# A retention layer feeding a squared-ReLU FFN on one core: the first four chunks and the first two weight pieces in another order

## The chip, the cores and the metric

The kernel runs on one core of one Trainium2 chip. The metric is the device time of one execution in microseconds (us), from the median of several runs. Everything below about engines comes from one profiled execution of that core: TensorE (PE, with its weight loads shown apart as PEld), VectorE (DVE), ScalarE (ACT), GpSimd (POOL), and SyncE (SP), which here only issues DMAs.

## What is computed

For 8 batches of 8 heads, 576 positions and head size 64, the reference computes retention without a softmax, and sends the result through a two-layer network:

```python
scores = (1/sqrt(64)) * q @ k.T                      # per batch and head
D[s, t] = gamma[h] ** (s - t) if s >= t else 0       # gamma[h] = 1 - 2 ** (-5 - h)
ret = (scores * D) @ v                               # (8, 8, 576, 64)
x = ret.transpose(0, 2, 1, 3).reshape(4608, 512)
h = maximum(x @ w_in, 0)                             # w_in (512, 2048)
out = (h * h) @ w_out                                # w_out (2048, 512)
```

q, k and v are float32. The two weights arrive as float64, so each must be turned into float32 on the chip before it is of use.

## The kernel before, in words

**Chunks.** The 4608 rows of x are made in 36 chunks of 128 rows (`C`). For each chunk q, k and v are loaded; q and v are multiplied by powers of gamma (`scale_q`, `scale_v`); q and k are turned around on PE by products with the identity (`turn_in`, L434) and copied out of PSUM by ACT or DVE (`turn_out`, L448, the copies on L454). `scores_full` (L503) makes the 128x128 scores of the eight heads with PE (L509) and multiplies them by the causal mask on DVE, one instruction for each half of the heads (L513); `carry_full` (L520) adds what earlier chunks left in a state (L529); `retain_full` (L532) multiplies the masked scores by v (L535) and k by v for the next state (L538), after which ACT copies the state (L501) and the chunk's x (L550). That is the form of chunks 0 to 3, the only ones that the change names. They are written out by hand at the end of the kernel, L853 to L914; the later ones run in the loop at L915. Each engine executes its own instructions in the order in which this Python text issues them, and so does the SP queue its DMAs. Nothing is reordered by a planner.

**Weight pieces.** w_in is cut into 16 pieces of 512x128. A piece comes in as 512 KB of raw float64 (`fetch_w`, L205; `fetch_raw(n)` fetches the next n, at most eight ahead), and is made float32 by six steps (`round_parts`, L219): *one* (L227), *two* (L231), *three* (L238), *four* (L241) and *five* (L244) on DVE, and *beside* (L235) on ACT, which needs *one* and is needed by *four*. `convert(n)` issues the next n of these steps, wherever the previous call stopped, in the order one, two, beside, three, four, five.

**The FFN of block 0.** Four chunks make a block of 512 rows. For block 0 the first layer is computed plainly: `first_in(j, halves, at)` (L667) multiplies piece j by the chosen rows of x (L677, four contraction steps, each of which shows as two PE instructions), ACT applies the ReLU (L683), and the square is queued: on ACT (L685) when both halves of the rows are taken, on DVE (L687) when only one is; `some(2)` in the next `first_in` issues it. Piece 0 is taken in four quarters of 128 rows, each as soon as a chunk's x is there; `N_HALF` says how many pieces are taken other than whole. What is left of block 0 waits in the list `steps`, and `step()` runs the next one. All other blocks go through seven products in place of eight (L717), and the second layer does likewise (L1061).

**Queues and buffers around the change.** In L152 to L158 a chunk's q and k come in two DMAs each (even heads, odd heads; 128 KB each), its v in one. Nearly all DMAs are issued from SP; `issue` (L149) sends k and v of chunk 0 through ACT's queue. PSUM holds a pool of three banks (tag f) that scores, first-layer products and warming products share in rotation, two banks for the turned q and k of the early chunks, one tile for x (`x_ps`, with one buffer, so that the next chunk's `carry_full` waits until L550 has read it) and one for the state. `warm(n)` issues products of no use into an f bank.

The order before, from L854 on, cut to its core:

```python
scale_q(1, nc.vector, halves); load(3); fetch_raw(3); warm(1)
scores_full(0); turn(1, (0, 0)); carry_full(0); retain_full(0); convert(3)
scores_full(1); scale_q(2, nc.gpsimd); carry_full(1); retain_full(1); convert(3)
turn(2, (0, 0)); load(4); ...; first_in(0, (0,), (0, C))
scores_full(2); scale_q(3, nc.gpsimd); carry_full(2); turn(3); retain_full(2)
```

Piece 0 was fetched earlier, at L345, between chunk 1's k and v; `load(2)` follows it.

Of the kernel before, what the change touches and what calls it, by code (L numbers as in the profile page):

```python
# [15 lines left out]
C = 128  # L16
CH = C // 2
TOK = 512
HT = TOK // 2
# [22 lines left out]
def kernel(  # L42
# [33 lines left out]
    nc = tc.nc  # L76
# [3 lines left out]
    HP = H // 2  # L80
# [59 lines left out]
    def load(i, names="qkv"):  # L140
        if i == 0:
            nc.sync.dma_start(dv, decays)
        got = loaded.setdefault(i, [None] * 3)
        for name, pool, src in (("q", ld3, q), ("k", ld5, k), ("v", ld4, v)):
            if name not in names:
                continue
            t = got["qkv".index(name)] = pool.tile([128, H, D], F32, tag=name, name=f"{name}_ld")

            issue = nc.scalar if i == 0 and name != "q" else nc.sync  # L149
            b, c0 = divmod(i * C, S)  # L150
            runs = [(b, c0, slice(0, C))] if c0 + C <= S else [(b, c0, slice(0, CH)), (b + 1, 0, slice(CH, C))]
            for e in range(1 if name == "v" else 2):  # L152
                for b, c0, to in runs:
                    at = src[b, :, c0:c0 + to.stop - to.start, :].rearrange("h s d -> s h d")
                    if name == "v":
                        issue.dma_start(t[to], at)
                    else:
                        issue.dma_start(t[to, e * HP:(e + 1) * HP, :], at[:, e::2, :])  # L158
# [5 lines left out]
    pieces = [(0, m, e) for m in range(N_M) for e in range(2)]  # L164
    pieces += [(1, mq + mh * N_MQ, e) for mq in range(N_MQ) for mh in range(2) for e in range(2)]
    N_W1 = N_DF
    N_HALF = 1
    stage = [W[5].rearrange("p (o s f) -> p o s f", o=4, s=NP),
             W[6][:, 0:3 * NP * 128].rearrange("p (o s f) -> p o s f", o=3, s=NP)]
    N_RAW = 8  # L170
# [11 lines left out]
    def rows(half, n=64):  # L182
        return slice(64 * half, 64 * half + n)
# [21 lines left out]
    def fetch_w(j):  # L205
        if j < len(pieces) and wide:
            to = raw_of(j).bitcast(I64)
            if pieces[j][0] == 0:
                nc.sync.dma_start(to.rearrange("p (c f) -> p c f", c=N_DM), piece_src(j))
                return  # L210
            to = to.rearrange("p (o s b c) -> o s p b c", o=2, s=2, b=4)
            for o in range(2):
                for s in range(2):
                    nc.sync.dma_start(to[o, s], piece_src(j)[o, s])
# [94 lines left out]
    def fetch_raw(count):  # L309

        for _ in range(count):
            if n_raw[0] < min(N_W1, n_made[0] + N_RAW):
                fetch_w(n_raw[0])
                n_raw[0] += 1
# [18 lines left out]
    def convert(count):  # L333
        for _ in range(count):
            f = next(w_in_steps, None)
            f and f()
# [44 lines left out]
    HEADS = [(hp, e, hp // (HP // 2)) for hp in range(HP) for e in range(2)]  # L381
# [10 lines left out]
    def scale_q(i, engine, parts=(slice(0, H),)):  # L392
        at = N_PAT + i % N_PAT
        for heads in parts:
            t = loaded[i][0][:, heads, :]
            engine.tensor_tensor(t, t, dv[:, heads, at:at + 1].to_broadcast(list(t.shape)), op=ALU.mult)  # L396
# [8 lines left out]
    def new_qk(i):  # L405
        t = work3.tile([128, 2, HP, C], F32, tag="qk", name="qk")
        st[i]["qT"], st[i]["kT"] = t[:, 0, :, :], t[:, 1, :, :]
        return t
# [22 lines left out]
            nc.scalar.copy(*moves.pop(0)[2:])  # L431
            count -= 1

    def turn_in(i, js=(1, 0)):  # L434

        if "p" not in st[i]:
            if i < N_EARLY:
                p = [ps_e.tile([128, 512], F32, tag=f"e{h}", name="t_ps") for h in range(2)]
            else:
                p = [ps_f.tile([128, 512], F32, tag="f", name="t_ps") for h in range(2)]  # L440
            st[i]["p"] = [x.rearrange("p (j d t) -> p j d t", j=2, d=HP) for x in p]
        for j in js:
            for hp in range(HP):
                for h in range(2):
                    nc.tensor.transpose(st[i]["p"][h][:, j, hp, :], loaded[i][j][rows(h), 2 * hp:2 * hp + 2, :],  # L445
                                        ident[rows(h), rows(h)])

    def turn_out(i, engines=(0, 1)):  # L448

        p = st[i].pop("p")  # L450
        to = new_qk(i)
        copies = (nc.scalar.copy, nc.vector.tensor_copy)
        for h in range(2):
            copies[engines[h]](to[:, :, :, CH * h:CH * h + CH], p[h])  # L454

    def turn(i, engines=(0, 1)):
        turn_in(i)
        turn_out(i, engines)
# [61 lines left out]
    def carry_full(i):  # L520

        xp[0] = ps_x.tile([128, 2, 256], F32, tag="x", name="x_ps", padded_shape=[128, 2, 512])
        clean.clear()
        if i == 0:
            u_ps[0] = ps_u.tile([128, HP, D], F32, tag="u", name="u_ps")
            return
        u = u_sb[2 * i % 3]
        for hp, e, b in HEADS[0:2] + HEADS[4:6] + HEADS[2:4] + HEADS[6:8]:
            nc.tensor.matmul(x_full(hp, e, b), lhsT=u[rows(e), hp, :], rhs=st[i]["qT"][rows(e), hp, :],  # L529
                             start=clears(b, e), stop=False, skip_group_check=True)  # L530

    def retain_full(i):  # L532

        for hp, e, b in (HEADS[j] for j in (0, 4, 2, 6, 1, 5, 3, 7)):
            nc.tensor.matmul(x_full(hp, e, b), lhsT=st[i]["vs"][:, head(hp, e), :], rhs=st[i]["ret"][:, e, hp, :],  # L535
                             start=clears(b, e), stop=False, skip_group_check=True)
        for hp, e, b in HEADS:
            nc.tensor.matmul(u_ps[0][rows(e), hp, :], lhsT=loaded[i][1][:, 2 * hp + e, :], rhs=st[i]["vs"][:, head(hp, e), :],  # L538
                             start=(i == 0 and hp == 0), stop=(hp == HP - 1), skip_group_check=True)
        x_out(i, lambda: grown(i, 1))  # L540
# [126 lines left out]
    def first_in(j, halves=(0, 1), at=(0, HT)):  # L667

        assert n_made[0] > j
        wi, m, e = pieces[j]  # L670
        mp, mm = divmod(m, 2)
        p = ps_f.tile([128, 2, HT], F32, tag="f", name="h_ps")
        w = w_in[mp][:, mm, 2 * e:2 * e + 2, :, :].rearrange("p s c f -> p (s c) f")
        lo, hi = halves[0], halves[-1] + 1
        p = p[:, lo:hi, at[0]:at[1]]
        for c in range(N_DM):
            nc.tensor.matmul(p, lhsT=w[:, c, :], rhs=xT[0][:, c, :].rearrange("p (h t) -> p h t", h=2)[:, lo:hi, at[0]:at[1]],  # L677
                             start=(c == 0), stop=(c == N_DM - 1))

        t = g_room[mp % 2][:, 2:5:2, mm, :] if e else g_room[mp % 2][:, 0:4:3, mm, :]  # L680
        t = t[:, lo:hi, at[0]:at[1]]
        some(2)
        nc.scalar.activation(t, p, AF.Relu)  # L683
        if hi - lo == 2:
            queue.append(lambda: nc.scalar.activation(t, t, AF.Square))  # L685
        else:
            queue.append(lambda: nc.vector.tensor_tensor(t, t, t, op=ALU.mult))  # L687
        if mm and e and hi == 2 and at[1] == HT:
            queue.append(lambda: [nc.sync.dma_start(
                g_dram[0, a:b, :, 2 * mp:2 * mp + 2, :].rearrange("s p m t -> p s (m t)"),  # L690
                g_room[mp % 2][:, a:b, :, :].rearrange("p s m t -> p s (m t)")) for a, b in QUARTERS])
        if j >= N_W1 - 4:

            sums_w.setdefault(0, sum_w_in(0)).pop(0)()
            if n_next[0] > 1:
                if 1 not in sums_x:
                    sums_x[1] = sum_x(1)
                sums_x[1].pop(0)()
# [89 lines left out]

    def block_steps(n):
        if n == 0:  # L790
            seconds = [(0, first_in, j, (1,), (C, HT)) for j in range(N_HALF)]
            return seconds + [(0, first_in, j) for j in range(N_HALF, N_W1)]
        return [(n, ffn_in, n, mp, j) for mp in range(N_MP) for j in range(NP)]

# [58 lines left out]
    halves = (slice(0, HP), slice(HP, H))  # L853
# [3 lines left out]
    scale_v(0)  # L857
    turn_in(0, (0,))
    turn_out(0)
    scale_q(1, nc.vector, halves)  # L860
    load(3)
    fetch_raw(3)
    warm(1)
    scores_full(0)
    turn(1, (0, 0))
    carry_full(0)
    retain_full(0)
    convert(3)
    scores_full(1)
    scale_q(2, nc.gpsimd)  # L870
    carry_full(1)
    retain_full(1)
    convert(3)
    turn(2, (0, 0))
    load(4)
    load(5, "qk")
# [3 lines left out]
    first_in(0, (0,), (0, C))  # L880
    scores_full(2)
    scale_q(3, nc.gpsimd)
    carry_full(2)
    turn(3)
    retain_full(2)
    load(6)
    fetch_raw(1)
    convert(3)
    scores_full(3)
    scale_q(4, nc.gpsimd)  # L890
    carry_full(3)
    first_in(0, (0,), (C, HT))
    early.close()
    ps_t[0] = first.enter_context(tc.tile_pool(name="ps_t", bufs=1, space=PS))
    convert(3)
    retain_full(3)
    first_in(0, (1,), (0, C))
    convert(6)
    scale_v(4)
    step()  # L900
    step()
# [239 lines left out]
    for k in range(N_K + 1):  # L1141
        j = k % NP
# [81 lines left out]
```

## Time and profile before

| what | value |
|---|---|
| median of three runs | 931.96 us (931.69 to 932.58) |
| the profiled execution's own time | 931.9 us |
| its span, first to last instruction | 930.2 us |
| PE busy | 922.4 us, 99% of the span |
| DVE busy | 755.4 us, 81% |
| ACT busy | 346.2 us, 37% |
| POOL busy | 82.9 us, 9% |
| granted PE clock | 0.999 of full |
| PE busy from 5.68 to 17.00 us | 9.75 of 11.32 us |
| PE busy from 17.00 to 31.40 us | 14.40 of 14.40 us |

The busy share of PE counts an instruction from its start to its modelled end; products overlap, so start-to-start distances say more than sums of durations. In the timeline a line gives the start, the time covered, the engine, the source line, the operation, what it writes and reads, shape, count, and in brackets the idle time of the engine ahead of it with what ended it. In the table of DMA issues the last column is the time from issue to landing.

### The profile page before, as it was taken

The numbers are of one execution on the slowest core, as the hardware profiler recorded it, in microseconds if no ns is written. First come the engines' busy times: TensorE is split into PE (matmuls) and PEld (weight loads), VectorE is DVE, ScalarE is ACT, GpSimd is POOL, SyncE is SP. The second block draws the span as 40 slices with busy tenths as digits, with TensorE's granted clock in tenths as the row PEclk, the third lists the DMA queues.
The fourth block names the chain that finished last, engine by engine and source line by source line (L and its number), as shares of the span: only waits on it lengthen the run. The fifth ranks groups of instructions, "written<-read, shape, count | busy, mean of one in ns | idle before, by whom it ended". The sixth has DMA issues, their size and how long they took to land.

```text
span 930.2 us, 21072 instructions
## 1 busy us (share of the span) xinstructions
PE 922.4 (99%) x8548; PEld 830.2 (89%) x8548; DVE 755.4 (81%) x1215; ACT 346.2 (37%) x788; POOL 82.9 (9%) x82
## 2 busy tenths in 40 slices
PE   8999999999999999999999999999999999999997
PEld 7654888888888888888888899999999999999997
DVE  5888788888898888979876587888888888877877
ACT  3457767667676676676711110000000000000000
POOL 3222111011111111211000000000000000000000
PEclk9999999999999999999999999999999999999999
DMA  9998657578666775784379996566666575465523
GB/s 226 220 270 218 166 153 202 161 214 267 167 180 184 259 216 146 223 271 137 114 258 355 383 318 193 145 176 191 168 180 183 156 206 155 114 178 142 151 79 68
DMA packets 297376, 181.29 MB, mean 195 GB/s; under 512 B 194368, under 2 KB 270272, under 8 KB 296384
## 3 DMA queue, kind: packets, MB, share of 16 engines
q1 hardware_dynamic: 292208, 178.84, 66.5%
q10 hardware_dynamic: 5072, 1.12, 0.6%
q8 instruction: 67, 1.10, 0.5%
q14 instruction: 29, 0.24, 0.1%
HBM read 109.39 MB, written 70.52 MB: 193 GB/s over the span
## 4 chain that ended last, share of the span: by engine, by line
PE 98%; DVE 1%; DMA 1%; SPq 0%; issue 0%; ACT 0%; DVEq 0%
PE h_b L717 18%; PE o_b L1061 18%; PE h_a L717 12%; PE h_c L717 12%; PE o_c L1061 12%; PE o_a L1061 12%; PE h_ps L677 6%; PE x_ps L574 3%; PE sc_ps L480 2%; PE x_ps L609 1%; PE u_ps L568 1%; DMA q_ld<-in_q_dram 1%; PE sc_ps L509 0%; PE t_ps L445 0%; PE x_ps L535 0%; DVE room L513 0%
## 5 line engine op out<-in xcount | busy, mean ns | idle before, releaser
L717 PE MATMUL h_b<-room,w 128*128 128x256 f32 x768 | 181.4, 379 | 0.0
L431 ACT COPY qk<-flip 32x256 f32<-32x256 f32 x432 | 173.8, 402 | 6.7
L717 PEld LDWEIGHTS h_b<-room,w 128*128 128x128 f32 x768 | 145.9, 190 | 19.8
L717 PE MATMUL h_a<-room,w 128*128 128x256 f32 x512 | 123.9, 385 | 0.0
L717 PE MATMUL h_c<-room,w 128*128 128x256 f32 x512 | 121.0, 379 | 0.0
L717 PEld LDWEIGHTS h_c<-room,w 128*128 128x128 f32 x512 | 97.3, 190 | 13.2
L717 PEld LDWEIGHTS h_a<-room,w 128*128 128x128 f32 x512 | 95.0, 190 | 13.7
L1061 PE MATMUL o_b<-room,w 128*128 128x192 f32 x496 | 90.8, 326 | 0.0
L1074 ACT COPY r<-o_a 128x192 f32<-128x192 f32 x28 | 8.9, 319 | 209.4 <-PE o_a L1061 209.4
L1061 PEld LDWEIGHTS o_b<-room,w 128*128 128x128 f32 x496 | 82.3, 190 | 0.0
L724 DVE SCALAR_TENSOR_TENSOR room<-room 128x512 f32<-128x512 f32 x96 | 66.7, 695 | 3.3
L396 POOL TENSOR_TENSOR q_ld<-q_ld,dv 128x512 f32<-128x512 f32 x34 | 37.7, 1110 | 286.1 <-DMA q_ld<-in_q_dram 257.2
L1061 PE MATMUL o_a<-a,w 128*128 128x192 f32 x352 | 62.6, 326 | 0.0
L1061 PE MATMUL o_c<-room,w 128*128 128x192 f32 x336 | 61.5, 326 | 0.0
L1061 PE MATMUL o_b<-s,w 128*128 128x192 f32 x336 | 61.5, 326 | 0.0
L1061 PE MATMUL o_c<-s,w 128*128 128x192 f32 x336 | 61.5, 326 | 0.0
L677 PE MATMUL h_ps<-room,w 128*128 128x512 f32 (+1 forms) x152 | 57.7, 532 | 0.7 <-DVE w L244 0.6
L1061 PEld LDWEIGHTS o_a<-a,w 128*128 128x128 f32 x352 | 58.1, 190 | 0.1
L1061 PE MATMUL o_a<-room,w 128*128 128x192 f32 x320 | 56.9, 326 | 0.0
L1061 PEld LDWEIGHTS o_c<-room,w 128*128 128x128 f32 x336 | 55.8, 190 | 0.0
L1061 PEld LDWEIGHTS o_b<-s,w 128*128 128x128 f32 x336 | 55.8, 190 | 0.0
L1061 PEld LDWEIGHTS o_c<-s,w 128*128 128x128 f32 x336 | 55.8, 190 | 0.0
(116 smaller groups left out, 1409.2 us busy)
## 6 DMA issues: line engine op xcount, KB each, us to landing
g_dram<-room SPq DMA_DIRECT2D x164, 256.0 KB, 3.8
a<-g_dram SPq DMA_DIRECT2D x30, 512.0 KB, 5.3
room<-g_dram SPq DMA_DIRECT2D x28, 512.0 KB, 5.0
w_dram<-w SPq DMA_DIRECT2D x28, 448.0 KB, 4.5
w<-w_dram SPq DMA_DIRECT2D x7, 1792.0 KB, 9.8
q_ld<-in_q_dram SPq DMA_DIRECT2D x64, 128.0 KB, 4.1
w<-in_moe_w_in_dram SPq DMA_DIRECT2D x16, 512.0 KB, 6.3
w<-in_moe_w_out_dram SPq DMA_DIRECT2D x64, 128.0 KB, 3.4
```

The source lines that it names most:

```text
L396: engine.tensor_tensor(t, t, dv[:, heads, at:at + 1].to_broadcast(list(t.shape)), op=ALU.mult)
L431: nc.scalar.copy(*moves.pop(0)[2:])
L480: nc.tensor.matmul(st[i]["sc"][e][rows(h), hp, :], lhsT=st[i]["kT"][rows(e), hp, t], rhs=st[i]["qT"][rows(e), hp, t], start=True, stop=Tru ...
L568: return [lambda hp=hp, e=e, b=b: nc.tensor.matmul(u[rows(e), hp, :], lhsT=loaded[i][1][rows(h), 2 * hp + e, :], rhs=st[i]["vs"][rows(h), ...
L574: return [lambda hp=hp, e=e, b=b: nc.tensor.matmul(x_at(hp, e, b, h), lhsT=s["vs"][rows(h), head(hp, e), :], rhs=s["ret"][rows(h), e, hp, ...
L609: m = nc.tensor.matmul(x_at(hp, e, b, h), lhsT=u[rows(e), hp, :], rhs=s["qT"][rows(e), hp, CH * h:CH * h + CH], start=clears(b, e), stop=F ...
L677: nc.tensor.matmul(p, lhsT=w[:, c, :], rhs=xT[0][:, c, :].rearrange("p (h t) -> p h t", h=2)[:, lo:hi, at[0]:at[1]], start=(c == 0), stop= ...
L717: nc.tensor.matmul(p[:, mm, :], lhsT=w[:, c, :], rhs=xs[n][right][:, c, :], start=(j in OPENS and mm == 0 and c == 0), stop=(j in CLOSES a ...
L724: nc.vector.scalar_tensor_tensor(t, t, 0.0, t, op0=ALU.max, op1=ALU.mult)
L1061: nc.tensor.matmul(p, lhsT=w_out[j][:, m, WO_SLOT[right], :], rhs=s["lefts"][left][:, m, :], start=(i in OPENS and m == 0), stop=(i in CLO ...
L1074: nc.scalar.copy(r[:, 0, LEFT], p)
```

## The change

1. Chunk 0's q is issued from ACT's queue and its k and v from SP's; before, it was the other way round.
2. Chunk 1's q is scaled half on DVE and half on GpSimd; before, both halves on DVE.
3. The raw piece 1 is fetched ahead of chunk 3's q, k and v; before, behind them. Pieces 2 and 3 stay behind.
4. Chunk 1's first half of the heads is turned around right after chunk 0's scores; the second half inside `retain_full(0)`, between the four products of the even heads and the four of the odd ones. Its copies are split between ACT and DVE; before, both on ACT.
5. Of piece 0, *one*, *two*, *beside* and *three* are issued inside `retain_full(0)` too, *four* and *five* after the mask of chunk 1.
6. All six steps of piece 1 are issued after the mask of chunk 2, ahead of `carry_full(2)`. Before, they came after the mask of chunk 3 and later.
7. Piece 0's second quarter goes between `carry_full(2)` and `retain_full(2)`; chunk 3 is turned around after `retain_full(2)`; piece 1 is used in two halves of 256 rows, the first ahead of `scores_full(3)`, the second as a step at the end; piece 0's third quarter goes ahead of `retain_full(3)`.

```diff
-            issue = nc.scalar if i == 0 and name != "q" else nc.sync
+            issue = nc.scalar if i == 0 and name == "q" else nc.sync
...
-    N_HALF = 1
+    N_HALF = 2
...
-    def turn_in(i, js=(1, 0)):
+    def turn_in(i, js=(1, 0), hps=range(HP)):
...
-            for hp in range(HP):
+            for hp in hps:
...
-    def retain_full(i):
-
-        for hp, e, b in (HEADS[j] for j in (0, 4, 2, 6, 1, 5, 3, 7)):
+    def retain_full(i, inside=lambda: None):
+
+        for j in (0, 4, 2, 6, 1, 5, 3, 7):
+            hp, e, b = HEADS[j]
+            if j == 1:
+                inside()
...
-            seconds = [(0, first_in, j, (1,), (C, HT)) for j in range(N_HALF)]
+            seconds = [(0, first_in, 0, (1,), (C, HT))] + [(0, first_in, j, (1,)) for j in range(1, N_HALF)]
...
-    scale_q(1, nc.vector, halves)
+    scale_q(1, nc.vector, halves[:1])
+    scale_q(1, nc.gpsimd, halves[1:])
+    fetch_raw(1)
     load(3)
-    fetch_raw(3)
+    fetch_raw(2)
     warm(1)
     scores_full(0)
-    turn(1, (0, 0))
+    turn_in(1, (1, 0), (0, 1))
     carry_full(0)
-    retain_full(0)
-    convert(3)
+    retain_full(0, lambda: [turn_in(1, (1, 0), (2, 3)), turn_out(1), convert(4)])
     scores_full(1)
     scale_q(2, nc.gpsimd)
+    convert(2)
     carry_full(1)
     retain_full(1)
-    convert(3)
     turn(2, (0, 0))
...
     scores_full(2)
     scale_q(3, nc.gpsimd)
+    convert(6)
     carry_full(2)
+    first_in(0, (0,), (C, HT))
+    retain_full(2)
     turn(3)
-    retain_full(2)
     load(6)
     fetch_raw(1)
-    convert(3)
+    first_in(1, (0,))
     scores_full(3)
     scale_q(4, nc.gpsimd)
+    convert(3)
     carry_full(3)
-    first_in(0, (0,), (C, HT))
+    first_in(0, (1,), (0, C))
     early.close()
...
     convert(3)
     retain_full(3)
-    first_in(0, (1,), (0, C))
-    convert(6)
     scale_v(4)
     step()
     step()
```

## The prediction, made before the changed kernel was run

> **What bounds the kernel now.** I read the page's busy times first, then PE's waits, then the timelines of PE, DVE, POOL and ACT over the first 55 us, and the DMA issues there.
>
> ```profile
> PE 922.4 (99%) x8548; PEld 830.2 (89%) x8548; DVE 755.4 (81%) x1215; ACT 346.2 (37%) x788; POOL 82.9 (9%) x82
> ```
>
> PE is the bound. PE's waits over the whole span, the four that the view lists (total, times, longest):
>
> ```profile
> PE idle_ps L845 <- DVE w L342: 1.1, 1, 1.1
> PE h_ps L677 <- DVE w L244: 0.6, 1, 0.6
> PE x_ps L535 <- DVE room L513: 0.4, 2, 0.3
> PE sc_ps L509 <- DVE qk L454: 0.3, 1, 0.3
> ```
>
> All of them lie ahead of 17 us. So whatever moves the start of the first step after the changed stretch, `turn(4)`, moves the end by as much, as long as no new wait appears behind it. PE's timeline gives the marks:
>
> ```profile
> 13.74 1.16 PE L535 MATMUL x_ps<-room,v_ld 128*64 128x128 f32 x16 [0.27 <-DVE room L513]
> 14.74 0.64 PE L538 MATMUL u_ps<-v_ld,k_ld 128*64 128x64 f32 x16
> 15.30 0.46 PE L445 MATMUL t_ps<-w,k_ld 64*128 64x64 f32 x8
> 15.60 0.41 PE L445 MATMUL t_ps<-w,q_ld 64*128 64x64 f32 x8
> 16.63 1.16 PE L677 MATMUL h_ps<-room,w 128*128 128x128 f32 x8 [0.61 <-DVE w L244]
> 17.71 1.16 PE L509 MATMUL sc_ps<-qk 64*128 64x128 f32 x16
> ...
> 31.41 0.46 PE L445 MATMUL t_ps<-w,k_ld 64*128 64x64 f32 x8
> ```
>
> The start of chunk 2's turning is 15.30, the one stall worth having is the 0.61 ahead of piece 0's first quarter (16.63, waiting for *five*, L244), and `turn(4)` starts at 31.41. Start to start, from this timeline: turning 0.65, scores 1.09, carry 0.60, a quarter of a piece 1.09, products with v 0.92, state 0.57; three groups (two quarters and a whole piece) take 25.80 to 31.41, so a whole piece is 5.61 - 2.18 = 3.43 and a half about 1.72.
>
> DVE, POOL and ACT show what a conversion costs undisturbed and disturbed:
>
> ```profile
> 28.01 1.06 POOL L396 TENSOR_TENSOR q_ld<-q_ld,dv 128x512 f32<-128x512 f32 x1 [7.36 <-DVE w L238]
> ```
>
> ```profile
> 18.91 1.29 DVE L513 TENSOR_TENSOR room<-sc_ps,room 128x512 f32<-128x512 f32 x2 [2.34 <-PE sc_ps L509]
> ...
> 28.05 1.57 DVE L241 SCALAR_TENSOR_TENSOR w<-w,w 128x512 f32<-128x512 f32 x1
> ...
> 49.38 0.41 DVE L227 TENSOR_SCALAR w<-w 128x512 uint32<-128x512 uint32 x1
> ...
> 51.69 0.69 DVE L244 SCALAR_TENSOR_TENSOR w<-w,w 128x512 uint32<-128x512 uint32 x1
> ```
>
> From 49.38 to 52.38 one piece takes 3.00 us with POOL idle. At 28.05 *four* takes 1.57 in place of 0.69, because POOL began at 28.01: it ends 0.55 after POOL does. The mask at 18.91 keeps its 1.29 although POOL works from 19.59 on.
>
> [...] It also shows a *one* (L227, 56.59) at 0.93 in place of 0.42 beside POOL, so I take all five DVE steps to be exposed. [...] issue to landing is 5 to 6 us from the fourth microsecond on, so the engines have a backlog and bytes decide. [...]
>
> **Part by part.**
>
> *q first, and chunk 1 around chunk 0 (edits 1, 2, 4).* In the landing times (start of the issue plus the last column of the DMA issues), chunk 0's k lands at 3.69 and 5.31, its q at 5.05 and 6.03, and the scaling (0.42) follows the last q. With q first, the scaling runs before k is complete. Bytes up to the last needed landing fall a little, and I expect the copies at 6.6 instead of 6.91, and chunk 1's scores at 11.3 instead of 11.71. SP gets one DMA more to issue (0.53 on ACT's queue); behind a backlog of 5 us that costs nothing, without the backlog 0.5 on everything from SP. But two things take the gain back before chunk 2. First, *beside* of piece 0 now stands on ACT ahead of the state copy and the x copy. It needs *one*, which needs piece 0: issued at 5.06, landed 5.9 later at 10.93.
>
> ```profile
> w<-in_moe_w_in_dram SPq DMA_DIRECT2D x1, 512.0 KB, 5.9
> ```
>
> *One* from 11.05 to 11.47, then on ACT 0.61 for *beside*, 0.27 and 0.59: x is read by 12.98, and `carry_full(1)`, which needs that PSUM tile, starts at 13.07, where chunk 1's scores were over at 12.4. After 0.60 of carry, chunk 1's products start at 13.7 as they do now. Second, chunk 2's second half of k is issued at 10.75 and takes this long:
>
> ```profile
> k_ld<-in_k_dram SPq DMA_DIRECT2D x1, 128.0 KB, 4.5
> ```
>
> That is 15.24; PE turns chunk 2 at 15.30 now. Nothing ahead of it in the byte order changes, so **chunk 2 is turned at 15.3 again**. These edits are worth 0 here (bounds: a gain of 0.2, since the first half of k2 is there at 13.9; a loss of 0.5 if SP's issues slip).
>
> *Piece 0 sooner (edit 5).* *Three* moves ahead of chunk 1's mask; behind the mask (13.9) come *four* and *five*, 0.7 each, with `scale_q(2)` on POOL until about 14.7: done at 15.95, where PE gets there. The quarter starts at 16.03: **-0.60**. Scores of chunk 2 need ACT's copies of the turned chunk, over at 17.25 as now (16.16 + 1.09): they start at 17.3, 0.41 earlier than 17.71. Carry 18.4, second quarter 19.0, products with v 20.1, state 21.0, turning of chunk 3 21.6, **PE reaches piece 1 at 22.2**.
>
> *Piece 1 ahead of chunk 3 (edit 3).* v of chunk 2 lands at 16.32. Now chunk 3 follows (q to 17.36, k to 18.51, v 19.52), then piece 1 (21.49, that is 1.97 for 512 KB). After: piece 1 at 18.3, q 19.3, k 20.5, v 21.5. k is in time for 21.6. But `scale_q(3)` and `scale_v(3)` on POOL, now at 17.52 and 19.59, move to 19.4-20.5 and 21.6-22.6.
>
> *Piece 1's conversion (edit 6).* Its six steps stand on DVE behind chunk 2's mask, which starts 1.20 after the scores (18.91 - 17.71) and lasts 1.27: 18.5 to 19.8. From there 3.00 undisturbed would end at 22.8. Both POOL instructions now fall inside: *one* starts at 19.8 while POOL works until 20.5 (+0.55), and `scale_v(3)` slips in between *three* and *four* (+0.88, as at 28.05). Piece 1 is ready at **24.2**, and PE waits from 22.2 to 24.25: **+2.05**. Bounds: both collisions missed 0.6, one 1.2, both with a bad start 2.4. On DVE the second copy of chunk 3 and chunk 3's mask are queued behind it; PE comes to them later than DVE does.
>
> *Piece 1 by halves (edit 7).* 2 x 1.72 against 3.43: 0 (bounds 0 and +0.3). Its squares go to DVE, two of some 0.45, and leave ACT (0.64). The rest of the edit is a new order of the same PE work.
>
> **Sum.** From piece 1 on: half 1.72, scores 1.09, carry 0.60, quarter 1.09, v 0.92, state 0.57, quarter 1.09, half 1.72 = 8.80. 24.25 + 8.80 = 33.05 for `turn(4)`, against 31.41: **+1.64**. Behind that, piece 2 is ready near 32.4 to 33.0 (mask of chunk 3 over at 28.4, 3.0 of conversion, one square, one or two collisions); PE wants it at 33.7. Later pieces have 1.0 to 4 us of slack and DVE has gaps (0.41, 0.88) to catch up. The profiled execution's own time is 931.9 (930.2 of span and 1.7 around it; the median is 931.96), so 931.9 + 1.64 = 933.5; I say **933.6**, in favour of small waits left out. That is slower, but by a hair under 0.2% (1.9 us, about what a measurement of this kernel can tell from no change).
>
> **Rivals.** *Piece 1 in time*: the collisions fall elsewhere, or chunk 3's loads land early. PE then waits 0 to 1.2: `turn(4)` between 31.0 and 32.25, so 931.5 to 932.8. For it: POOL's spans are rough. Against it: v of chunk 3 can't land much ahead of 21.5, and any landing between 19.8 and 23.4 collides. *DVE late a second time*: the forecast's wait, plus piece 2. DVE has taken two squares more and stands 1 us later relative to PE; if piece 2 is ready after 33.7, each tenth beyond counts; with chunk 4's `scale_v` (POOL at 31.95 now) inside *five* and one more delay I put it at +1, so 934.7, clearly slower. Against it: 0.7 of slack. *A front that gains more*: if k2's landing moved too and all four waits vanished, up to 2 us, 929.9. Against it: the byte order.
>
> **How the numbers follow.** Forecast 0.50 (933.0 to 934.2, of that 0.20 above 933.8), piece 1 in time 0.26, late twice 0.18, front 0.06 with half of it under 930.0. With a little of the second rival's lower edge: faster 0.06, slower 0.20 + 0.18 and a rest, 0.40, same 0.54. Range 931.4 to 934.8: it leaves out the front case and the tail of the late one.
>
> **What would show it.** Right: piece 0's quarter at 16.0 with hardly a wait; chunk 2 turned at 15.3; a wait of about 2 us of PE for L244 near 22 to 24, with two DVE steps stretched beside POOL; `turn(4)` near 33.0. Wrong: no such wait, chunk 2 turned well before 15, or a new wait behind 31 us.

## The result, and the profile after

| what | before | after |
|---|---|---|
| median of four runs, side by side | 932.07 us | 936.40 us (935.64 to 937.71) |
| ratio, 95% interval | | 1.0047 (1.0034 to 1.006) |
| the profiled execution's own time | 931.9 us | 935.64 us |
| its span | 930.2 us | 933.9 us |

The change makes the kernel slower by some 4.3 us. The forecast was 933.6 us, its range 931.4 to 934.8, so the result lies above the range. The profiled execution is the fastest of the four; what the median has above it, 0.76 us, lies outside this profile.

The page's busy times of the changed kernel:

```profile
PE 922.4 (99%) x8556; PEld 831.5 (89%) x8556; DVE 760.3 (81%) x1217; ACT 345.0 (37%) x787; POOL 84.5 (9%) x83
```

PE is busy for 922.4 us, exactly as before, and the span is 3.7 us longer. The whole difference is therefore PE waiting. The view of PE's waits of the changed kernel (total, times, longest) names it:

```profile
PE h_ps L680 <- DVE w L244: 1.8, 1, 1.8
PE idle_ps L848 <- DVE w L342: 1.1, 1, 1.1
PE h_ps L680 <- ACT room L553: 1.0, 1, 1.0
PE u_ps L571 <- ACT u_sb L501: 0.9, 1, 0.9
PE x_ps L529 <- ACT room L553: 0.6, 1, 0.6
```

(From `retain_full` on, the changed kernel's lines stand 3 further down: L677 became L680, L550 became L553.) The second line stood there before. The first is the wait that was forecast, for *five* of piece 1. The third and the fourth are new and were not forecast. The fifth, of `carry_full(1)` for ACT, was in the forecast. PE's timeline of the changed kernel gives their places:

```profile
13.08 0.67 PE L529 MATMUL x_ps<-qk,u_sb 64*64 64x128 f32 x16 [0.57 <-ACT room L553]
...
15.17 0.46 PE L445 MATMUL t_ps<-w,k_ld 64*128 64x64 f32 x8
...
15.81 1.16 PE L680 MATMUL h_ps<-room,w 128*128 128x128 f32 x8
17.18 1.16 PE L509 MATMUL sc_ps<-qk 64*128 64x128 f32 x16 [0.21 <-ACT qk L454]
...
24.01 1.97 PE L680 MATMUL h_ps<-room,w 128*128 128x256 f32 x8 [1.85 <-DVE w L244]
25.90 1.16 PE L509 MATMUL sc_ps<-qk 64*128 64x128 f32 x16
...
29.60 0.63 PE L541 MATMUL u_ps<-v_ld,k_ld 128*64 128x64 f32 x16
31.25 2.89 PE L680 MATMUL h_ps<-room,w 128*128 128x128 f32 x16 [1.01 <-ACT room L553]
34.07 0.46 PE L445 MATMUL t_ps<-w,k_ld 64*128 64x64 f32 x8
...
58.96 0.27 PE L571 MATMUL u_ps<-v_ld,k_ld 64*64 64x64 f32 x2 [0.94 <-ACT u_sb L501]
```

Chunk 2 is turned 0.13 us earlier than before (15.17 against 15.30), `turn(4)` 2.66 us later (34.07 against 31.41). Matching steps of PE then stay some 2.55 us late up to 54 us, 3.72 us late from 59 us on, and nothing is gained or lost from there to the end. So the loss is made in two places: 2.6 us between 22 and 34 us, and 1.2 us at 59 us.

**The wait for piece 1.** DVE and POOL in the changed kernel, in their timelines:

```profile
18.37 1.29 DVE L513 TENSOR_TENSOR room<-sc_ps,room 128x512 f32<-128x512 f32 x2 [2.64 <-PE sc_ps L509]
19.58 1.03 DVE L227 TENSOR_SCALAR w<-w 128x512 uint32<-128x512 uint32 x1
...
21.77 1.36 DVE L241 SCALAR_TENSOR_TENSOR w<-w,w 128x512 f32<-128x512 f32 x1
23.17 0.69 DVE L244 SCALAR_TENSOR_TENSOR w<-w,w 128x512 uint32<-128x512 uint32 x1
```

```profile
19.26 1.06 POOL L396 TENSOR_TENSOR q_ld<-q_ld,dv 128x512 f32<-128x512 f32 x1 [1.73 <-DMA q_ld<-in_q_dram]
21.29 1.29 POOL L495 TENSOR_TENSOR v_ld<-v_ld,dv 128x512 f32<-128x512 f32 x1 [0.97 <-DMA v_ld<-in_v_dram]
```

*One* takes 1.03 us where 0.41 was seen undisturbed, *four* 1.36 where 0.69 was: 0.62 and 0.67 us, each beside one of the two scalings of chunk 3 on POOL. *Five* starts at 23.17 and ends at 23.86, and PE, which got there at 22.16 (24.01 less 1.85), goes on at 24.01.

**The fourth quarter's wait.** ACT in the changed kernel:

```profile
30.34 0.37 ACT L501 COPY u_sb<-u_ps 128x256 f32<-128x256 f32 x1 [0.70 <-PE u_ps L541]
30.61 0.59 ACT L553 COPY room<-x_ps 128x512 f32<-128x512 f32 x1
```

The fourth quarter of piece 0 reads chunk 3's rows of x. ACT copies them at L553, behind the state at L501, which can't be copied before PE's products of k and v (29.60) are done. PE is over with those at about 30.2 and stands until 31.25. Before, the third quarter stood between `retain_full(3)` and the fourth: 1.09 us of PE that needs nothing of chunk 3. PE and ACT of the kernel before:

```profile
25.80 5.68 PE L677 MATMUL h_ps<-room,w 128*128 128x128 f32 x24
```

```profile
26.24 0.59 ACT L550 COPY room<-x_ps 128x512 f32<-128x512 f32 x1
```

The first 1.09 us of the PE line are the third quarter, so the fourth began at 26.89, just behind the end of the copy (26.83). Edit 7 moves the third quarter ahead of `retain_full(3)`, and the copies lie open.

**The state copy near 59 us.** DVE, POOL and ACT of the changed kernel there:

```profile
54.17 1.43 DVE L244 SCALAR_TENSOR_TENSOR w<-w,w 128x512 uint32<-128x512 uint32 x1
55.52 1.28 DVE L227 TENSOR_SCALAR w<-w 128x512 uint32<-128x512 uint32 x1
```

```profile
53.83 1.22 POOL L495 TENSOR_TENSOR v_ld<-v_ld,dv 128x512 f32<-128x512 f32 x1 [6.90 <-DMA v_ld<-in_v_dram]
55.02 1.50 POOL L396 TENSOR_TENSOR q_ld<-q_ld,dv 128x512 f32<-128x512 f32 x1
```

```profile
56.83 0.72 ACT L235 ACTIVATE w<-w,exp_bias 128x512 uint32<-128x512 uint32 x1 [2.79 <-DVE w L227]
57.46 0.61 ACT L688 ACTIVATE room<-room 128x512 f32<-128x512 f32 x1
57.98 0.57 ACT L686 ACTIVATE room<-h_ps 128x512 f32<-128x512 f32 x1
58.46 0.36 ACT L501 COPY u_sb<-u_ps 128x256 f32<-128x256 f32 x1
```

Read it from the top. Two scalings in a row on POOL hold up *five* of one piece (1.43 in place of 0.69) and *one* of the next (1.28 in place of 0.42), 1.60 us together. *Beside* waits on ACT for that *one*. Behind *beside* in ACT's order stand a square, a ReLU and the state copy, none of which needs what *beside* makes. Before, the same copy ran here:

```profile
54.73 0.37 ACT L501 COPY u_sb<-u_ps 128x256 f32<-128x256 f32 x1
```

PE needed it at 55.24, so it was over in time. With everything 2.55 us later it would come at 57.28; it comes at 58.46, 1.18 us later than that, and PE goes from 2.55 to 3.72 us late.

### The profile page after: what moved, and what is told of

The parts are those of the page before. It is cut to its first block, busy times and chain, and to the rows that moved or that the text cites. A ratio compares the mean times of both kernels' runs of the same rounds, so it can differ in the third digit from the quotient of the medians.

```text
span 933.9 us, 21089 instructions
## 1 busy us (share of the span) xinstructions
PE 922.4 (99%) x8556; PEld 831.5 (89%) x8556; DVE 760.3 (81%) x1217; ACT 345.0 (37%) x787; POOL 84.5 (9%) x83
## 4 chain that ended last, share of the span: by engine, by line
PE 96%; DVE 2%; ACT 1%; issue 0%; DVEq 0%; ACTq 0%
PE h_b L720 18%; PE o_b L1066 18%; PE h_a L720 12%; PE h_c L720 12%; PE o_c L1066 12%; PE o_a L1066 12%; PE h_ps L680 5%; PE x_ps L577 3%; PE sc_ps L480 2%; PE x_ps L612 1%; PE u_ps L571 1%; PE idle_ps L848 0%; PE t_ps L445 0%; DVE w L238 0%; DVE w L244 0%; PE sc_ps L509 0%
## 5 line engine op out<-in xcount | busy, mean ns | idle before, releaser
L396 POOL TENSOR_TENSOR q_ld<-q_ld,dv 128x512 f32<-128x512 f32 (+1 forms) x35 | 39.3, 1124 | 285.9 <-DMA q_ld<-in_q_dram 215.6
L680 PE MATMUL h_ps<-room,w 128*128 128x512 f32 (+2 forms) x160 | 58.0, 514 | 2.9 <-DVE w L244 1.8
```

## The experiments

All ratios are to the kernel before, run beside the experiment on the same chip.

**The third quarter put back behind `retain_full(3)`.**

```diff
     carry_full(3)
-    first_in(0, (1,), (0, C))
     early.close()
...
     retain_full(3)
+    first_in(0, (1,), (0, C))
     scale_v(4)
```

> The changed kernel, with piece 0's third quarter put back behind retain_full(3), where it stood before. Theory A (the loss is a sum of separate new waits of PE: 1.85 us for piece 1, 1.01 for chunk 3's x ahead of the fourth quarter, 0.94 for a state copy near 59 us): the 1.01 goes, and since nothing stands between the carry and the products with v of chunk 3 any more, 0.3 to 0.5 for chunk 3's mask comes in its place; the time is 0.5 to 0.7 us below the changed kernel's. Rival (VectorE's lateness is the one cause, and the wait for x only an image of it): a wait of about 1 us stays ahead of the fourth quarter or just behind it, and the time does not move.

Measured: 934.42 us, ratio 1.0029 (1.0018 to 1.004). The wait of 1.01 us is gone; another, of 0.27 us for POOL at 28.15, has come up. From piece 1 to `turn(4)` PE takes 9.38 us (24.23 to 33.61) in place of 10.06 (24.01 to 34.07). The order of one quarter thus costs 0.68 us in the changed kernel. The median is lower by more, 2.0 us (1.4 below the repeat of the changed kernel further down). In the profiled execution the wait near 59 us is absent as well, which is of this size; one profile doesn't tell how often.

**Piece 1 without POOL beside it.** The scaling of chunk 3's q and v is left out.

```diff
-        if i:
+        if i == 3:
+            st[i]["vs"] = loaded[i][2]
+        elif i:
             scale_v(i)
...
     scores_full(2)
-    scale_q(3, nc.gpsimd)
     convert(6)
```

> The changed kernel without scale_q(3) and scale_v(3): it leaves out the scaling of chunk 3's q and v by the powers of gamma, so no GpSimd instruction runs beside the conversion of piece 1. Theory A (those two instructions hold up VectorE): one and four take 0.42 and 0.69 us again, piece 1 is ready 1.2 us sooner, PE waits about 0.6 us for it in place of 1.85, and the time is 1.2 us below the changed kernel's, or about 2 if the late state copy near 59 us goes with it. Rival (piece 1 is late because its conversion stands behind chunk 2's mask, whatever GpSimd does): the wait stays above 1.4 us.

Measured: 933.35 us, ratio 1.0013 (1.0005 to 1.0022). PE's waits (the lines stand 2 further down):

```profile
PE h_ps L682 <- ACT room L555: 1.0, 1, 1.0
...
PE h_ps L682 <- DVE w L244: 0.6, 1, 0.6
```

Of the 1.85 us, 0.57 are left: 1.28 us were the two collisions (0.62 + 0.67 on DVE's rows above), and 0.57 is that six steps behind the mask of chunk 2 are too late for that place in PE's order even undisturbed. The fourth quarter's wait is untouched, so it has another cause. `turn(4)` starts at 32.90.

**The front alone** (edits 1, 2, 4 and 5; the fetch order and all from the turning of chunk 2 on as before).

```diff
-    N_HALF = 2
+    N_HALF = 1
...
-    fetch_raw(1)
     load(3)
-    fetch_raw(2)
+    fetch_raw(3)
...
     scores_full(2)
     scale_q(3, nc.gpsimd)
-    convert(6)
     carry_full(2)
-    first_in(0, (0,), (C, HT))
-    retain_full(2)
     turn(3)
+    retain_full(2)
...
```

> The front edits alone: chunk 0's q first, chunk 1's q scaled on two engines, chunk 1 turned around chunk 0's products, piece 0 converted sooner; everything from turn(2) on, the fetch order and the use of piece 1 are as before. Theory A (the front gains 0.5 to 0.8 us at piece 0's first quarter, the loss lies in the back): chunk 2's scores start near 17.2 us where they started at 17.71, no wait of PE appears behind 17 us, and the time is 0.4 to 0.6 us below the kernel before: 931.5. Rival (the front's new queueing on ScalarE and SyncE shifts transfers and costs more later): a new wait behind 30 us, and the time is at or above that of before.

Measured: 931.94 us, ratio 0.9995 (0.9987 to 1.0003), no difference that can be told. It is not that nothing is gained. Piece 0's first quarter starts at 15.63 (16.63 before), and `turn(4)` at 30.70 (31.41), 0.71 us earlier. PE's waits show why it is not more, and where it goes:

```profile
PE t_ps L445 <- DMA k_ld<-in_k_dram: 0.8, 2, 0.4
...
PE sc_ps L480 <- DVE qk L454: 0.2, 1, 0.2
```

A PE that is early meets k before it has landed, twice, for 0.8 us together (chunk 0's at 5.58, chunk 1's at 8.66); that wait did not exist before. From chunk 2's scores to `turn(4)` the lead is 0.71 us. Then chunk 4's scores take 1.16 us from start to start (35.09 to 36.25) in place of 0.63, in the middle of which PE waits for DVE's copy of the turned chunk. The lead falls from 0.71 to 0.18 us, and 0.10 is left at the end.

**The rest alone** (edits 3, 6 and 7; the front as before).

```diff
-            issue = nc.scalar if i == 0 and name == "q" else nc.sync
+            issue = nc.scalar if i == 0 and name != "q" else nc.sync
...
-    turn_in(1, (1, 0), (0, 1))
+    turn(1, (0, 0))
     carry_full(0)
-    retain_full(0, lambda: [turn_in(1, (1, 0), (2, 3)), turn_out(1), convert(4)])
+    retain_full(0)
+    convert(3)
     scores_full(1)
     scale_q(2, nc.gpsimd)
-    convert(2)
     carry_full(1)
     retain_full(1)
+    convert(3)
```

> The back edits alone: piece 1 fetched ahead of chunk 3, converted ahead of carry_full(2), used by halves, and the new order from turn(2) on; chunk 0 and chunk 1 as before. Theory A: piece 1's wait of about 1.5 to 2 us and the wait of 1.0 us for chunk 3's x are there, and the front's gain of 0.5 is not: 0 to 1 us above the changed kernel, 936 to 937.5. Rival (the loss needs the front's earlier start): within 1 us of the kernel before.

Measured: 934.63 us, ratio 1.003 (1.002 to 1.004), lower than expected. `turn(4)` starts at 34.02, 2.61 us late, and PE stays 2.50 us late to the end: the waits for piece 1 (1.41, beside 0.54 for piece 0) and for the fourth quarter are there in full, the one near 59 us is not.

```profile
PE h_ps L680 <- DVE w L244: 1.9, 2, 1.4
...
PE h_ps L680 <- ACT room L553: 1.0, 1, 1.0
```

So the first 2.6 us belong to these three edits and come with or without the front. (Edits 6 and 7 were not run apart from each other.) The extra wait near 59 us does not follow from them every time.

**The front, with ACT making the copies of `turn(4)`**, and **the same with *beside* of piece 0 later**.

```diff
-    turn(4)
+    turn(4, (0, 0))
```

```diff
-    retain_full(0, lambda: [turn_in(1, (1, 0), (2, 3)), turn_out(1), convert(4)])
+    retain_full(0, lambda: [turn_in(1, (1, 0), (2, 3)), turn_out(1), convert(2)])
+    convert(2)
```

> The front edits alone, and both copies of turned chunk 4 on ScalarE (turn(4, (0, 0))), where VectorE made one. In the front-only run the 0.7 us gained up to turn(4) shrank to 0.2 at chunk 4's scores, which waited for VectorE's copy behind a conversion. Theory A (that copy is what takes the gain back): chunk 4's scores start 0.6 to 0.7 us ahead of the kernel before, and the time is 931.4, some 0.5 us below it. Rival (VectorE is late by itself, and whatever comes next in its order takes the copy's place): the gain is given back within the next two pieces, and the time is that of the front-only run, 931.9.

> As the front edits with both of chunk 4's copies on ScalarE, and piece 0's beside (with three) issued behind chunk 0's state copy and x copy, where the change has it ahead of them. Theory A (beside ahead of the copies costs the 0.57 us wait of chunk 1's carry): that wait goes, but chunk 1's products with v then wait for VectorE's mask and GpSimd's scale_v(1) instead, so chunk 2 is turned only 0.0 to 0.3 us sooner than in the front-only run (14.99) and the time falls by at most 0.3. Rival (the wait is lost in full): chunk 2 is turned at 14.4, and the time falls by 0.5.

Measured: 931.73 us, 0.9997 (0.9989 to 1.0005), and 931.69 us, 0.9995 (0.9987 to 1.0003). Neither can be told from the kernel before. The first says little on its question: its profiled execution lost 0.77 us at the masks of chunks 0 and 1 (0.51 and 0.26), so `turn(4)` came at 31.49 and there was no lead left to keep, though nothing was lost at chunk 4's scores either. In the second the wait of `carry_full(1)` for ACT (0.57) is gone and chunk 2 is turned at 14.65 in place of 14.99, but 0.39 us of waiting for the scaled v of chunk 1 took its place, and the lead is given back afterwards in small waits for k, a mask and the state copy. Each stall taken away at the front uncovers another a few tenths behind it.

**The changed kernel again, and with ACT making the copies of `turn(4)`** (the same line edited in the changed kernel).

> The changed kernel once more, unaltered, because its four times spread over 2 us and the profiled one was the lowest. Theory A (the waits for piece 1 and for chunk 3's x are there in every execution, 2.7 us at turn(4); the wait near 59 us depends on where GpSimd's instructions meet VectorE's): turn(4) again at 33.9 to 34.2, the wait near 59 us anything from 0 to 3 us. Rival (one fixed loss of 3.7 us): the same waits to 0.2 us.

> The changed kernel with both copies of turned chunk 4 on ScalarE, which takes 0.7 us from VectorE at 36 us. Theory A (the wait for a state copy near 59 us comes from VectorE running late): it shrinks or goes, turn(4) stays at 34.0, and the time is 934.6 to 935.4 in place of 936.4. Rival (VectorE's lateness there is set by loads and GpSimd alone): the wait and the time stay.

Measured: 935.83 us, ratio 1.0037 (1.0023 to 1.0051), and 937.84 us, 1.0059 (1.004 to 1.0079). The repeat shows the first two waits as before, and another one:

```profile
PE h_ps L680 <- DVE w L244: 1.8, 1, 1.8
PE u_ps L571 <- issue: 1.3, 1, 1.3
...
PE h_ps L680 <- ACT room L553: 1.0, 1, 1.0
```

Over eight executions the changed kernel took 934.93 to 937.71 us. Up to `turn(4)` these two profiles agree (+2.66 and +2.71), near 60 us they don't: 0.94 us for ACT in one, 1.33 us for nothing that the profile shows in the other. The last experiment shows that the part up to `turn(4)` isn't the same in every execution either.

For the second kernel the expectation failed. Its profiled execution took 940.61 us, and the windows of 1 us show something that no wait lists. (The columns are the stretch, its length, busy time of PE, PEld, DVE, ACT and POOL, granted PE clock, DMA share, GB/s.) First this kernel, then the changed one:

```profile
24.00:25.00 1.00, 1.00 (x5) 0.90 (x6) 0.78 (x2) 0.00 (x0) 0.00 (x0) 0.93 1.13 155
25.00:26.00 1.00, 1.00 (x4) 0.81 (x3) 0.00 (x0) 0.00 (x0) 0.00 (x0) 0.50 0.72 121
```

```profile
25.00:26.00 1.00, 1.00 (x7) 0.62 (x5) 0.00 (x0) 0.00 (x0) 0.00 (x0) 1.00 0.77 131
```

PE is busy in both, but at 0.50 of its clock in the first. The half clock begins at 24.9, after a wait for piece 1 of 2.10 us in place of 1.85, and the windows show it up to 28.00, for 3.1 us at least. It came once more at 62.4, behind two waits of 0.88 and 1.08 us, and lasted 3.4 us (a clock of 0.90 from 60 to 63 us, 0.50 to 65, 0.59 to 66). `turn(4)` was 4.20 us late. That can't come from the line edited, which acts behind `turn(4)`. What the line is worth is thus not shown by this run; it shows that the wait for piece 1 may have an edge behind it.

**Piece 1 later**, to test that edge: six small fills of `idle` on DVE between *four* and *five*.

```diff
-    convert(6)
+    convert(5)
+    for _ in range(6):
+        nc.vector.memset(idle, 1.0)
+    convert(1)
```

> The changed kernel with six short fills of an unused 128x128 tile on VectorE ahead of piece 1's last conversion step: nothing but a delay of 0.7 to 1.0 us of piece 1. Theory A (piece 1's lateness reaches PE one for one, and a PE wait of about two microseconds or more can halve PE's granted clock for one stretch of 3.4 us, as in the profile of the changed kernel with both copies on ScalarE, where the wait was 2.10 us): the wait before piece 1 is 2.6 to 2.9 us, a stretch of half clock follows it at once, and turn(4) comes at 36.0 to 36.8 in place of 34.1. Rival (the half clock came from elsewhere): the clock stays whole and turn(4) comes at 34.8 to 35.1.

Measured: 938.24 us, ratio 1.0067 (1.005 to 1.0083). PE waits 2.49 us, 0.64 more than in the changed kernel, and `turn(4)` comes at 36.86, 2.79 later. Of that, 0.59 was lost ahead of piece 1 (PE reached it at 22.75, mostly for chunk 1's mask), 0.64 is the longer wait, and the remaining 1.56 arose behind it. PE's timeline and the windows:

```profile
25.24 2.54 PE L680 MATMUL h_ps<-room,w 128*128 128x256 f32 x8 [2.49 <-DVE w L244]
27.71 2.08 PE L509 MATMUL sc_ps<-qk 64*128 64x128 f32 x16
```

```profile
20.00:25.00 5.00, 2.75 (x54) 2.42 (x52) 4.39 (x12) 2.24 (x5) 1.59 (x2) 1.00 1.07 272
25.00:28.00 3.00, 2.76 (x10) 1.92 (x12) 1.09 (x4) 0.18 (x1) 1.06 (x1) 0.75 0.46 90
28.00:31.00 3.00, 3.00 (x37) 2.60 (x37) 1.18 (x2) 0.21 (x1) 0.41 (x1) 0.68 0.96 199
31.00:40.00 9.00, 7.99 (x75) 5.92 (x75) 8.69 (x15) 3.50 (x8) 3.79 (x4) 1.00 1.09 253
```

A clock of 0.75 over 3 us is 1.5 us at one half, 0.68 over 3 us another 1.9: 3.4 us in all, in which the scores of chunk 3 take 2.08 us in place of 1.16. That is where the 1.56 us are. By the same figures the half clock begins near 26.5, some 1.3 us after PE has gone on, not at once as expected. The longer wait and then the half clock thus come together without the edit of `turn(4)`. But one of the four executions kept a mean clock of 1.0 and took 937.63 us all the same. It left no trace, so either its wait was shorter or such a wait doesn't bring the half clock every time; and the clock isn't all of this kernel's loss.

**The fetch order alone** (edit 3 on the kernel before).

```diff
-    load(3)
-    fetch_raw(3)
+    fetch_raw(1)
+    load(3)
+    fetch_raw(2)
```

> The kernel before with one edit: raw piece 1 is fetched ahead of chunk 3, pieces 2 and 3 behind it. Theory A (bytes decide, so chunk 3 lands 2 us later): chunk 3's k is whole at 20.3 in place of 18.5, and PE, which turns chunk 3 at 19.4 in this order, waits 0.9 to 1.2 us; piece 1's own wait stays away; the time is 0.9 to 1.3 above that of before, 933.2. Rival (the slack of the loads covers it): no wait, the time is unchanged.

Measured: 932.88 us, ratio 1.001 (1.0002 to 1.0019). Chunk 3's k lands at 19.72 and 20.29 in place of 17.94 and 18.51, and PE, which in the order of before turns chunk 3 ahead of `retain_full(2)`, waits for it:

```profile
19.85 0.82 PE L445 MATMUL t_ps<-w,k_ld 64*128 64x64 f32 x8 [0.50 <-DMA k_ld<-in_k_dram]
```

`turn(4)` is 0.81 us late, the end 1.0. So the 512 KB put ahead cost chunk 3's k behind them 1.8 us of landing time; edit 7, which turns chunk 3 after `retain_full(2)`, covers this in the changed kernel.

**The collisions near 54 us taken away.** The scaling of chunk 7's v and chunk 8's q is left out of the changed kernel.

```diff
     def scale_q(i, engine, parts=(slice(0, H),)):
+        if i == 8:
+            return
...
         vs = st[i]["vs"] = loaded[i][2]
+        if i == 7:
+            return
```

> The changed kernel without scale_v(7) and scale_q(8): it leaves out the scaling of chunk 7's v and chunk 8's q, the two GpSimd instructions that met VectorE's conversions at 53.8 and 55.0 us. Theory A (those two made one and with it beside and the state copy late near 59 us): no wait of PE for the state copy near 59 us, turn(4) still at 34.1, and the time 934.7 to 935.1, one to two below the changed kernel's. Rival (VectorE is late there by its own backlog): a wait of at least 0.5 us stays.

Measured: 935.38 us, ratio 1.0038 (1.0023 to 1.0053). No wait stands near 59 us: from 48 to 58 us each *five* takes 0.69 and each *one* 0.42, *beside* starts at 55.87 in place of 56.83, and PE's lag is level from 43 us on (3.86, at the end 3.7). This profile alone would not settle it, since PE is also some 1.3 us later here and so needs the copy later. The seven other profiles with edits 3, 6 and 7 do. In each of them the two scalings stretch two DVE steps near 54 to 58 us (1.43 and 1.28 in the changed kernel, 1.28 twice in the repeat, 1.59 and 1.43 with the copies of `turn(4)` on ACT). What differs is where these steps stand to the *one* whose *beside* is ahead of the state copy:

- *Five* and that *one* itself in the changed kernel: a wait of 0.94 us. *Four* and *five* ahead of it with the copies of `turn(4)` on ACT: 0.88 us. The same two with the fills, where PE is later too: some 0.3 us, too little for the list of waits.
- Only that *one* ahead, *two* behind it: the repeat, where PE loses some 0.2 us.
- Both behind that *one*: *three* and *four* with the third quarter put back, *two* and *three* in the rest alone, *four* and *five* without the scaling of chunk 3. No wait in any of the three.

So the chain collision, DVE, *beside*, state copy holds in every profile. DVE and POOL of the repeat show how little decides:

```profile
54.01 0.69 DVE L244 SCALAR_TENSOR_TENSOR w<-w,w 128x512 uint32<-128x512 uint32 x1
54.62 1.28 DVE L227 TENSOR_SCALAR w<-w 128x512 uint32<-128x512 uint32 x1
```

```profile
54.03 1.58 POOL L495 TENSOR_TENSOR v_ld<-v_ld,dv 128x512 f32<-128x512 f32 x1 [6.46 <-DMA v_ld<-in_v_dram]
```

POOL starts just behind *five* here, and *five* goes free; in the changed kernel's first profile it started 0.2 us sooner (53.83), ahead of *five* (54.17).

The time of this run is above what was expected, because PE lost 1.1 us at chunk 1's mask near 15 us, where the changed kernel's profile lost nothing (the lines stand 4 further down):

```profile
PE x_ps L542 <- DVE room L517: 1.8, 2, 1.1
```

DVE's timeline has the cause. Edit 5 puts *three* of piece 0 ahead of that mask, and in this execution the scalings of chunk 1's v and chunk 2's q on POOL stretch *two* and *three* (1.29 and 1.43 us). The changed kernel, its repeat and five of the variants (this one, third quarter back, no scaling of chunk 3, `turn(4)` copied by ACT, fills) are the same program up to 17 us. In three of these seven profiles PE waits for the mask, 1.13, 0.35 and 0.28 us; these are the three in which *three* takes 1.43 to 1.51 us in place of 0.69. With the third quarter put back:

```profile
14.16 1.16 PE L538 MATMUL x_ps<-room,v_ld 128*64 128x128 f32 x16 [0.35 <-DVE room L513]
```

Chunk 2 is turned between 14.84 and 16.89 us in the seven. So edit 5 brings a loss of its own in some executions.

## Why the prediction was wrong, step by step

The sign and the main mechanism were right, the size was not: 936.4 in place of 933.6 us, with two waits missing from the sum of the profiled execution.

| step | predicted | measured, profiled execution |
|---|---|---|
| `carry_full(1)` starts, behind *beside* on ACT | 13.07 | 13.08 |
| chunk 2's second half of k lands | 15.24 | 14.2 |
| chunk 2 turned | 15.3 | 15.17 |
| piece 0's first quarter starts | 16.03 | 15.81 |
| scores of chunk 2 | 17.3 | 17.18 |
| PE reaches piece 1 | 22.2 | 22.16 |
| wait for piece 1 | 2.05 | 1.85 |
| *one* and *four* held up by POOL | 0.55 and 0.88 | 0.62 and 0.67 |
| piece 1's first half to `turn(4)` | 8.80 | 10.06 |
| `turn(4)` | 33.05 | 34.07 |
| from `turn(4)` to the end | 0 | +1.1 |

- **The front** came out within a quarter of a microsecond at each mark of PE. Of the two reasons given for its worth of 0, the first stood: *beside* ahead of the copies on ACT takes 0.57 us of PE back. The second did not. Chunk 2's second half of k was to land at 15.24 again. In the changed kernel it is issued at 10.41 in place of 10.75 and lands 3.8 us later in place of 4.5, at 14.2, and no profile of the changed front shows a wait of PE for it at chunk 2. So 15.3 came out with one of its two reasons gone, and in part by luck: *three* ahead of chunk 1's mask was priced at nothing, and other executions turn chunk 2 as late as 16.89. The run of the front alone adds that what is gained up to `turn(4)`, 0.71 us, is mostly returned at chunk 4's scores.
- **The wait for piece 1** was right in place, cause and size: 1.85 us, of which 1.28 go with the two scalings on POOL. That *four* is held up beside a scaling the prediction had from the trace of before (1.57 in place of 0.69 at 28.05), and it came again (1.36 us). That *one* is exposed too it took from there as well (0.93 in place of 0.42 at 56.59), and it holds (1.03 and 1.28 us). *Two*, *three* and *five*, which it counted in, were held up elsewhere: 1.28 us at 55.82 in the repeat, 1.54 at 45.93 and 1.43 at 54.17 in the changed kernel. Why a scaling on POOL holds these steps up, no run shows.
- **Piece 1 by halves** was put at 0 with a bound of 0.3. The first half takes 1.89 us from start to start in place of 1.72: 0.17. Whether halving or the start after a wait costs that was not told apart.
- **The step that failed** is the sentence "The rest of the edit is a new order of the same PE work." The order was summed as durations of PE alone. What was not asked is which of the steps now stand directly behind what they read. The fourth quarter does: 1.01 us, the larger part of 10.06 - 8.80. With the third quarter put back that wait is gone, and 0.68 us of the stretch with it, since another wait of 0.27 us came up there.
- **A second step failed**: "Later pieces have 1.0 to 4 us of slack and DVE has gaps (0.41, 0.88) to catch up." PE never waits for a later piece, so the slack was there. But the lateness of DVE did not pass through a piece. It went through *beside* to ACT, whose order holds the state copy that PE needs. The rival *DVE late a second time* had named two collisions in a row, and a price of 1 us, but for piece 2 at 33.7 us; it came by another way, 25 us further on, for 1.17 us. It is also what the prediction named as a sign of being wrong, a new wait behind 31 us. The upper end of the range, 934.8, held the forecast and one such loss on top of it (+1, so 934.7), but had no room for the 1.01 us of the fourth quarter besides.
- **A clock of one half** after the wait was in no case. It did not occur in the profiled execution of the changed kernel. In two of the other three its mean granted clock is 0.997 in place of 1.0, which fits a stretch of the kind (the profiled execution with the fills has one, and 0.997 too); but the slowest, at 937.71 us, has 1.0, so the clock doesn't explain the median.

Settled are thus 1.85 us for piece 1 and 1.01 for the fourth quarter, in each of the two profiles of the changed kernel, and that the wait near 59 us depends on which DVE steps the scalings meet. What stays open: why v lands some tenths sooner or later from one execution to the next, how the 0.76 us between the profiled execution and the median divide between the mask of chunk 1, the half clock and the part near 60 us, and what PE waited for in the 1.33 us without a releaser.

## What to carry to other kernels

When work is moved to another place in an engine's order, ask of the step that comes *first behind the hole* what it reads, and who makes it: the third quarter was worth 1.09 us of cover for two copies on ACT as long as it stood between them and their reader. Follow a late engine through the queues of the engines that wait for it, not only to its own products; what stands behind a waiting instruction there may belong to someone else (here a state copy, for 1.17 us). A collision of two engines costs what stands behind the step that it hits, so 0.2 us in the start of one can decide between a wait of 0.94 us and one of 0.2. A stall removed at the front is worth only what the next landing or copy behind it leaves over (0.71 us at `turn(4)` was 0.10 at the end in the front alone), so read the slack of the following waits before counting a gain.

## What the runs showed of the hardware

PE's granted clock fell to 0.50 after PE had waited for 2.10 and 2.49 us, 0.9 and 1.3 us after it had gone on, and stayed there for at least 3.1 us in the first case and for 3.4 us in the second. It fell for 3.4 us behind two waits of 0.88 and 1.08 us near 60 us as well. In the two profiles of the changed kernel, with waits of 1.85 and 1.8 us for piece 1, it stayed at 1.0. Whether there is a limit between 1.85 and 2.10 us, and what besides the length of a wait decides, was not tried: the two shorter waits stand against a limit of that kind, and one of the four executions with the fills kept a mean clock of 1.0. The stretch cost 1.56 us where piece 1 was delayed by the fills.

POOL's scaling took longer as well where a DVE step that it collides with was under way as it started. By POOL's own spans, which the legend of the profile calls rough, the 128x512 product took 1.06 us at 19.26, but 1.29 us at 21.29, where *three* (20.98 to 21.67) was under way, and 1.50 us at 55.02, where *five* (54.17 to 55.60) was.
